# Two K tiles of a two-layer decode kernel come by strided transfers of 64 to 8 rows

## The chip, the cores and the metric

The kernel runs on one core of a Trainium2 chip. The time is that of the device, in microseconds (us), from one launch. The core has five engines with instruction queues of their own: TensorE (PE), VectorE (DVE), ScalarE (ACT), GpSimd (POOL) and SyncE (SP), and 16 DMA engines that carry transfers between the chip's memory and the core's SBUF of 128 partitions. In this kernel SP issues every transfer.

## What is computed

Two layers with the same weights are run for one new token in each of B = 2 sequences. A layer is a cached attention and then an MLP mixer:

```python
x = x + _A_ref(_layernorm(x), K, V, wq, wo)
x = x + _B_ref(_layernorm(x), w1, w2, w3, w4)

def _A_ref(x, k_cache, v_cache, wq, wo):          # D = 576, H = 32, Dh = 128, Sk = 16384
    q = (x @ wq).reshape(B, 1, H, Dh).transpose(0, 2, 1, 3)
    scores = einsum("bhqd,bhkd->bhqk", q, k_cache) * Dh ** -0.5
    o = einsum("bhqk,bhkd->bhqd", softmax(scores), v_cache)
    return o.transpose(0, 2, 1, 3).reshape(B, 1, H * Dh) @ wo
```

The mixer `_B_ref` is a layer norm, a D x D product and gelu, a shift along a sequence of length one, a second D x D product, and then a layer norm, D x 4608, gelu and 4608 x D. All data are bfloat16. The K and V caches are the bulk: for each of the 64 pairs of sequence and head there is a K and a V of 16384 x 128 values, 4 MB each, and both layers read the same caches.

## The kernel before

**Tiles.** One pair (b, h) is a unit u = 0..63. Its K is one tile, its V another. A tile of 4 MB is laid on the 128 partitions as `(p j) d -> p (j d)`: partition p gets rows 128p to 128p + 127 of the cache, which is one run of 32 KB in memory and 32 KB in SBUF. SBUF holds six such tiles (`NSLOT`, `TILE`) in the tensor `mem`. Some tiles at the ends of a layer are cut along the columns into pieces, and a few tiles of layer 0 stay in SBUF for layer 1 (`CARRY`).

**Transfers.** `plan_all` (L499) makes one list, in the order in which the transfers will be issued: wq and w2, the tiles of layer 0 in the order K0, K1, V0, K2, V1, ... (`tile_order`, L569), the weights wo, w3, w4, wq, the tiles of layer 1, and the last weights with w1. `plan_tile` (L426) and `plan_piece` (L435) put a tile on this list with its slot, its semaphore and a list of (destination, source) pairs; one pair is one transfer:

```python
        sem = f"tile{base // self.TILE}" if n == self.NB else f"piece{base // self.TILE}_{a}_{n}"
        self.store.plan((t, u, a, n), sem, base + 256 * a, 256 * n,
                        [(lambda m: m, src[:, a * 128:(a + n) * 128])])
```

`Store.pump` (L286) takes the list's head whenever its place in SBUF is free. It issues in order and never passes a transfer whose place is still in use. `Graph.dma` (L88) makes of each pair one `dma_start` on SP, all pairs of one tile on the same semaphore (L101); a reader waits for the sum, 16 for each transfer. So SP's queue is: wait until PE has read the tile that was in the slot before, issue, go on to the next tile.

**Compute.** For each unit, in turn: K arrives; PE transposes 64 of its 128 columns of blocks in chunks of eight (L1241), ACT copies them out of PSUM (L1253), PE multiplies by q (L1267); DVE does the other 64 blocks by a multiplication and a sum (L1287, L1291). DVE and POOL find the maximum, ACT takes the exponential (L1319, L1322), and PE multiplies by V one unit later (L1361). PE, ACT and DVE run most of this in loops of three units; SP's and POOL's queues are written out. POOL relays the landing of a tile to PE and DVE (L202). Between the layers the weights come in small pieces through two slots, each waiting for PE to have used the one before.

Of the kernel before, what the change touches and what calls it, by code (L numbers as in the profile page):

```python
# [328 lines left out]
class KB:  # L329
# [11 lines left out]
    PARKED = 5  # L341
    GONE = 72
    RAW = 2
    TURNS = {("w3", 0): 1, ("w3", 1): 1, ("w3", 2): 1, ("w4", 1): 1, ("w4", 3): 1, ("w4", 6): 1, ("w4", 8): 1,
             ("wq", 0): 1, ("wq", 1): 1, ("wq", 2): 1}

# [25 lines left out]
    def _alloc(self):  # L372
# [44 lines left out]
        self.quad = misc[:, 20:24]  # L417
        self.raw = misc[:, 24:24 + self.RAW * (1 + 3 * B) // 2].bitcast(BF16).rearrange("p (k c) -> p k c", k=self.RAW)
        self.cor = [self.prod[:, 1280 + 2 * MT * B * i:1280 + 2 * MT * B * (i + 1)].bitcast(FP32) for i in range(2)]
# [3 lines left out]
        self.mps = ps("mps", [128, 512], FP32)  # L423


    def plan_tile(self, t, u, slot, cuts=(), skip=0):  # L426

        b, hh = u % self.B, u // self.B
        src = (self.K if t == "k" else self.V)[b, hh].rearrange("(p j) d -> p (j d)", p=128)
        cuts = [0, *cuts, self.NB]  # L430
        for a, z in zip(cuts[:-1], cuts[1:]):
            if a >= skip:
                self.plan_piece(t, u, slot * self.TILE, src, a, z - a)

    def plan_piece(self, t, u, base, src, a, n):  # L435
        sem = f"tile{base // self.TILE}" if n == self.NB else f"piece{base // self.TILE}_{a}_{n}"
        self.store.plan((t, u, a, n), sem, base + 256 * a, 256 * n,
                        [(lambda m: m, src[:, a * 128:(a + n) * 128])])

    def plan_cols(self, nm, l, w, parts):  # L440

# [57 lines left out]
    def plan_all(self):  # L499

        T, U, n = self.TILE, self.U, self.KT - 1
        row, w3r, wqr = 2 * self.D, 2 * self.F, 2 * 128 * self.H
        H, MT = self.H, self.MT
        self.parts = {}
        self.plan_cols("wq", 0, self.wq, self.whole(self.wq, [4 * T + wqr * k for k in range(self.KT)]))
        self.plan_small("w2", 0, self.w2, 4 * T + wqr * n + wqr // 2, (0, 64))

        tiles = self.tile_order(0)
        place = [i % 6 for i in range(len(tiles))]
        place[-1] = 2  # L510
        half, quarter = self.BP, self.BP // 2
        for (t, u), slot in zip(tiles, place):
            self.plan_tile(t, u, slot, (half, half + quarter) if (t, u) == ("v", U - 1) else ())
        last = {tile: slot for tile, slot in zip(tiles, place)}
        third = U - self.CARRY - 1
        assert last["k", third] == 1 and last["v", third] == 4

        self.cuts = {}
        P = 4 * row
        a, c = [4 * T + P * i for i in range(4)], [T, T + P]  # L520
        assert 256 * self.GONE == 4 * P and 256 * 8 * self.PARKED >= 2 * P and 256 * 8 * self.NKT >= P
        turn = iter([*a, c[0]] + [a[0], a[1], c[1], a[2], a[3], c[0]] * 6)
        h = MT // 2
        self.cuts["wo", 0] = [(i, i + 4, next(turn)) for i in range(0, 32, 4)]
        halves = lambda n: [(k, m, z, next(turn)) for k in range(self.KT - 1) for m, z in ((0, n), (n, 2 * n))] + \
                           [(self.KT - 1, 0, 2 * n, next(turn))]
        w3 = halves(h)
        self.groups = [(0, 4, 8, 12, 16, 18), (0, 8, 12, 16, 18)]
        g = self.groups[0]
        self.cuts["w4", 0] = [(h * i + p, h * i + q, next(turn)) for i in range(2) for p, q in zip(g[:-1], g[1:])]  # L530
        self.plan_rows("wo", 0, self.wo, self.cuts["wo", 0])
        self.plan_cols("w3", 0, self.w3, w3)
        self.plan_groups("w4", 0, self.w4, self.cuts["w4", 0])
        self.plan_cols("wq", 1, self.wq, halves(H // 2))

        b, hh = third % self.B, third // self.B
        tiles = self.tile_order(1)
        b2, h2 = tiles[0][1] % self.B, tiles[0][1] // self.B
        for i in (1, 2, 3, None, 0):
            if i is None:  # L540
                self.plan_piece(*tiles[0], T, self.K[b2, h2].rearrange("(p j) d -> p (j d)", p=128), 0, quarter)
            else:
                self.plan_piece("v", third, 4 * T, self.V[b, hh].rearrange("(p j) d -> p (j d)", p=128),
                                i * self.GONE // 4, self.GONE // 4)
        place = [(3, 4, 5, 0, 2, 1)[i % 6] for i in range(len(tiles))]
        for i, (t, u) in enumerate(tiles):
            if (t, u) != ("v", third):
                self.plan_tile(t, u, place[i], (quarter, half, half + quarter) if i == 0 else
                               (half,) if i == len(tiles) - 1 else (), 0 if i else quarter)
        self.cuts["wo", 1] = [(0, 11, 2 * T), (11, 22, 2 * T + 11 * row), (22, 32, 0)]  # L550
        at = 10 * row
        w4_at = T + 2 * w3r + w3r // 2
        self.cuts["w4", 1] = [(0, 8, w4_at)] + \
                             [(a, b, 3 * T + (a - 8) * row) for a, b in ((8, 16), (16, 26), (26, 30), (30, 34), (34, 36))]
        self.plan_rows("wo", 1, self.wo, self.cuts["wo", 1])
        self.plan_cols("w3", 1, self.w3, self.whole(self.w3, [at, at + w3r, T, T + w3r, T + 2 * w3r]))
        self.plan_groups("w4", 1, self.w4, self.cuts["w4", 1])
        w1_at = 2 * T
        for i, k in enumerate((0, 2)):
            self.store.plan(("w1", 1, i), f"w1_{i}", w1_at + k * row, 2 * row, [  # L560
                (lambda m: m.rearrange("p (k n) -> p k n", n=self.D),
                 self.w1[k * 128:(k + 2) * 128, :].rearrange("(k p) n -> p k n", p=128))])
        self.store.plan(("w1", 1, 2), "w1_2", w1_at + 4 * row, row, [(lambda m: m[self.TL:, :], self.w1[4 * 128:, :])])
# [168 lines left out]
    def unscaled(self):  # L732

        R, B = self.RAW, self.B
        hi, lo = self.raw[:, :, 1:1 + B], self.raw[:, :, 1 + B:1 + 2 * B]
# [4 lines left out]
    def cols_chunk(self, w, l, k, out, pk, n, rhs, rk, cols, first, last=False, held=False):  # L740
# [15 lines left out]
        if l == (1 if w == "wq" else 0):  # L756
            self.turn(self.TURNS.get((w, k), 0), settle=not held)

# [60 lines left out]
    def hs_projection(self):  # L819
# [16 lines left out]
        self.copy_psum(self.hs, "hs")  # L836
        B, R = self.B, self.RAW
        self.dv(lambda e: e.tensor_copy(out=self.raw[:, :, 1 + 2 * B:], in_=self.hs[:, 0:R, :]),
# [22 lines left out]
    def rows_projection(self, w, l, rhs, rk):  # L861
# [4 lines left out]
        for i, (a, b, _) in enumerate(cuts):  # L866
# [14 lines left out]
            if l == 0:  # L881
                if (w, i) == ("wo", 1):
                    self.park(self.order(0)[self.U - self.CARRY - 1], self.NKT, self.PARKED)
                self.turn(self.TURNS.get((w, i), 0))

    def z_projection(self, l):
        B, KT, MT, R = self.B, self.KT, self.MT, self.RAW
        MB, w = MT * B, 1 + 3 * B
# [568 lines left out]
```

## Time and profile before

| | |
|---|---|
| median of 3 runs | 2550.42 us (2550.4 to 2551.58) |
| profiled execution | 2549.84 us, its span 2548.1 us |
| read from memory | 1092.37 MB, 429 GB/s over the span |
| busy share of the span | PE 63%, PE weight loads 62%, DVE 74%, ACT 47%, POOL 2% |
| transfers by size | 124 K tiles and 123 V tiles of 4096 KB, 76 smaller ones |
| issue to landing, median | K tile 40.7 us, V tile 49.6 us |

The profile page is of one execution. Its second part cuts the span into 40 slices of 63.7 us, with a digit for each engine (tenths busy), the share of the 16 DMA engines and the GB/s they moved. Its fourth part follows the chain of work that ended last back from the end: a "DMA" step there is from a transfer's issue to its landing. A row with SPq is an instruction of SP's queue that issues a transfer: start, duration, line, engine, form, what goes where. In a table of windows each engine has its busy us and count, then the granted TensorE clock, the share of the DMA engines and GB/s.

### The profile page before, as it was taken

Reading aid. Unit: us, or ns where it says so; the run is one execution under the profiler, and the core shown is the slowest. Engines: PE = TensorE matmul, PEld = TensorE weight load, DVE = VectorE, ACT = ScalarE, POOL = GpSimd, SP = SyncE. Lnnn points to the kernel's source line nnn. Section 1 sums busy time; section 2 is a strip of 40 time slices with the busy share of each in tenths; the row PEclk is TensorE's granted clock in tenths of the full one; section 3 lists DMA queues with packets and bytes.
Section 4 is the critical chain, followed back from the end, with each engine's and each line's share of the span. In section 5 each row is a group of like instructions: output and inputs, shape, how many; then the busy total and the mean of one; then the engine's idle time right before and its main releaser. Section 6 shows DMA issues by size and latency. Waiting matters only on the chain.

```text
span 2548.1 us, 74893 instructions
## 1 busy us (share of the span) xinstructions
PE 1614.7 (63%) x34407; PEld 1580.7 (62%) x34407; DVE 1897.0 (74%) x2062; ACT 1204.2 (47%) x1810; POOL 53.5 (2%) x151
## 2 busy tenths in 40 slices
PE   4666666656666666666777766656665666666566
PEld 3666666656666665666667666656665665666566
DVE  5877777777777777777648877777777777777774
ACT  3544544444454444445435544444454444445442
POOL 0000000000000000000000000000000000000000
PEclk8555555555555555555656555565555555555555
DMA  9999999999999999999999999999999999999999
GB/s 410 428 433 431 432 432 431 433 431 433 430 432 432 432 432 431 433 431 432 419 411 427 432 431 432 432 432 432 432 432 432 432 432 432 432 433 431 433 431 386
DMA packets 46928, 1093.19 MB, mean 429 GB/s; under 512 B 5140, under 2 KB 6296, under 8 KB 12440
## 3 DMA queue, kind: packets, MB, share of 16 engines
q1 hardware_dynamic: 46872, 1092.40, 100.0%
q8 instruction: 41, 0.67, 0.1%
q14 instruction: 15, 0.12, 0.0%
HBM read 1092.37 MB, written 0.00 MB: 429 GB/s over the span
## 4 chain that ended last, share of the span: by engine, by line
DMA 66%; DVE 23%; PE 5%; issue 5%; SPq 1%; ACT 0%; DVEq 0%; POOLq 0%
DMA mem<-in_A_k_cache_dram 63%; DVE s_dve L1291 12%; DVE prod L1287 9%; PE tps L1241 2%; PE mps L1361 2%; DMA mem<-in_B_w_dram 1%; DMA mem<-in_A_wo_dram 1%; PE sps L1267 1%; SPq L101 1%; PE sps L1212 1%; DVE diag L1208 0%; DVE l L1339 0%; DVE q_col L1205 0%; DMA mem<-in_A_wq_dram 0%; DVE mx L1302 0%
## 5 line engine op out<-in xcount | busy, mean ns | idle before, releaser
L1253 ACT ACTIVATE kt<-tps 128x1024 bf16<-128x1024 bf16 x992 | 1002.9, 1023 | 878.0 <-PE tps L1241 859.5
L1291 DVE TENSOR_REDUCE s_dve<-prod 128x16 f32<-128x2048 bf16 x504 | 1152.1, 2286 | 17.3
L1241 PE MATMUL tps<-ident,mem 128*128 128x128 bf16 x8192 | 1000.0, 300 | 141.3 <-POOLq L202 135.2
L1287 DVE TENSOR_TENSOR prod<-mem,qb 128x2048 bf16<-128x2048 bf16 x504 | 616.8, 1224 | 525.4 <-POOLq L202 493.9
L1361 PE MATMUL mps<-p,mem 128*128 128x1 bf16 x16384 | 512.2, 166 | 549.7 <-POOLq L202 519.3
L1241 PEld LDWEIGHTS tps<-ident,mem 128*128 128x128 bf16 x8192 | 761.3, 136 | 151.1 <-POOLq L202 145.0
L1361 PEld LDWEIGHTS mps<-p,mem 128*128 128x128 bf16 x16384 | 487.5, 104 | 558.3 <-ACT p L1322 552.2
L1267 PEld LDWEIGHTS sps<-q_col,kt 128*128 128x128 bf16 x7936 | 399.5, 113 | 0.8 <-ACT kt L1253 0.4
L1267 PE MATMUL sps<-q_col,kt 128*128 128x1 bf16 x7936 | 388.1, 170 | 0.4 <-issue 0.3
L1212 PE MATMUL sps<-diag,ones_bf 128*128 128x128 bf16 x127 | 36.5, 287 | 195.4 <-DVE diag L1208 195.4
L1212 PEld LDWEIGHTS sps<-diag,ones_bf 128*128 128x128 bf16 x127 | 13.2, 104 | 205.6 <-DVE diag L1208 205.6
L1316 ACT ACTIVATE mx<-mx 128x1 f32<-128x1 f32 x128 | 26.0, 203 | 236.2 <-POOL mx L1307 236.2
L1307 POOL PARTITION_ALL_REDUCE mx<-mx x128 | 51.1, 400 | 2441.9 <-DVE mx L1305 2323.7
L1215 ACT ACTIVATE qb<-sps 128x128 bf16<-128x128 f32 x127 | 35.2, 277 | 137.3 <-PE sps L1212 137.3
L1319 ACT ACTIVATE p<-s_dve,mx 128x64 bf16<-128x64 f32 x126 | 43.8, 348 | 4.1
L1253 ACT ACTIVATE mem<-tps 128x1024 bf16<-128x1024 bf16 x32 | 32.0, 1025 | 22.0 <-PE tps L1241 19.6
L1322 ACT ACTIVATE p<-sps,mx 128x64 bf16<-128x64 f32 x128 | 37.7, 294 | 0.1
L1302 DVE TENSOR_REDUCE mx<-sps 128x1 f32<-128x64 f32 x128 | 27.6, 216 | 7.5 <-PE sps L1267 7.5
L874 PE MATMUL mps<-prod,mem 128*128 128x2 bf16 x680 | 22.1, 166 | 14.5 <-DMA mem<-in_B_w_dram 8.8
L1208 DVE TENSOR_SCALAR diag<-ident,q_f 128x128 bf16<-128x128 bf16 x127 | 31.1, 245 | 0.0
L874 PEld LDWEIGHTS mps<-prod,mem 128*128 128x128 bf16 x680 | 20.6, 105 | 16.2 <-DMA mem<-in_B_w_dram 7.5
L707 ACT ACTIVATE misc<-misc 128x2 f32<-128x2 f32 x8 | 2.4, 296 | 51.4 <-DVE misc L705 51.4
(117 smaller groups left out, 293.4 us busy)
## 6 DMA issues: line engine op xcount, KB each, us to landing
mem<-in_A_k_cache_dram SPq DMA_DIRECT2D x124, 4096.0 KB, 40.7
mem<-in_A_v_cache_dram SPq DMA_DIRECT2D x123, 4096.0 KB, 49.6
mem<-in_B_w_dram SPq DMA_DIRECT2D x21, 576.0 KB, 7.7
mem<-in_B_w_dram SPq DMA_DIRECT2D x7, 1152.0 KB, 33.9
mem<-in_A_v_cache_dram SPq DMA_DIRECT2D x3, 2048.0 KB, 40.4
mem<-in_A_wq_dram SPq DMA_DIRECT2D x10, 512.0 KB, 6.5
mem<-in_A_wo_dram SPq DMA_DIRECT2D x8, 576.0 KB, 19.3
mem<-in_A_wq_dram SPq DMA_DIRECT2D x4, 1024.0 KB, 8.0
```

The lines of the kernel that those rows point to most:

```text
L874: ins = pe.matmul(self.mps[:, t * B:(t + 1) * B], lhsT=buf[:, o:o + 128], rhs=rhs(k), start=(k == 0 and t == 0), stop=(k == last), skip_gr ...
L1212: self.pe(lambda pe: pe.matmul(qps, lhsT=self.ones_bf[:, :], rhs=self.diag[:, :], start=True, stop=True, skip_group_check=True), reads=["o ...
L1215: self.act(lambda e: e.activation(out=self.qb[i][:, :], in_=qps, func=ACT.Copy), reads=[("qps", i)], writes=[("qb", i)], sig=("qb", i))
L1241: ins = pe.transpose(self.tps[t][:, j * 128:(j + 1) * 128], buf[:, j * 128:(j + 1) * 128], self.ident[:, :])
L1253: self.act(lambda e: e.activation(out=out, in_=self.tps[t][:, :], func=ACT.Copy), reads=[("tps", t)], writes=keys, sig=("evac", c, t, k))
L1267: ins = pe.matmul(self.sps[sp][:, c * self.CH + j:c * self.CH + j + 1], lhsT=buf[:, j * 128:(j + 1) * 128], rhs=self.q_col[:, sp:sp + 1], ...
L1287: self.dv(lambda e: e.tensor_tensor(out=prod, in0=buf.rearrange("p (j d) -> p j d", d=128), in1=qbc, op=ALU.mult), reads=[("qb", r)] + key ...
L1291: self.dv(lambda e: e.tensor_reduce(out=sd[:, c0:c0 + DB], in_=prod, axis=AX.X, op=ALU.add), reads=["prod"], writes=[("s_dve", r)], sig=(" ...
L1307: self.pool(lambda e: e.partition_all_reduce(mx[3], mx[2], channels=128, reduce_op=ROP.max), reads=[("mx2", i)], writes=[("mx3", i)])
L1319: self.act(lambda e: e.activation(out=p[:, n:self.NB], in_=self.s_dve[i][:, 0:self.NB - n], func=ACT.Exp, bias=mx[4], scale=self.scale, ac ...
L1322: self.act(lambda e: e.activation(out=p[:, 0:n], in_=self.sps[i][:, 0:n], func=ACT.Exp, bias=mx[4], scale=self.scale, accum_out=self.ls[:, ...
L1361: ins = pe.matmul(self.mps[:, 448:449], lhsT=buf[:, j * 128:(j + 1) * 128], rhs=p[:, col:col + 1], start=b == 0, stop=b == self.NB - 1, sk ...
```

## The change

Two of the tiles get a number, their share: K of unit 40 in layer 0 has 2, K of unit 20 in layer 1 has 1. A tile with a share no longer comes by one transfer of its 128 rows (partitions) but by several, each of evenly spaced rows. `runs` makes the list: rows in steps of 2, 4 and 8 (64, 32 and 16 rows) as the binary digits of 8 - share say, and what is left as runs of eight rows with a step of 16.

- Share 2: 64 rows with step 2 from 0, 32 rows with step 4 from 1, and 8 rows with step 16 from 3, 7, 11 and 15. Six transfers.
- Share 1: 64 rows with step 2 from 0, 32 rows with step 4 from 1, 16 rows with step 8 from 3, and 8 rows with step 16 from 7 and 15. Five transfers.

The first one waits for the slot as before; the others follow on SP without a wait. All of them count on the slot's semaphore. Every row goes to the partition that it went to before, and nothing changes on PE, DVE, ACT and POOL. By the change's own words half of the DMA engines move ten (nine) rows of such a tile and half six (seven), instead of eight each.

```diff
+    SHARE = {(0, "k", 40): 2, (1, "k", 20): 1}
...
-    def plan_tile(self, t, u, slot, cuts=(), skip=0):
+    def plan_tile(self, l, t, u, slot, cuts=(), skip=0):
...
             if a >= skip:
-                self.plan_piece(t, u, slot * self.TILE, src, a, z - a)
+                self.plan_piece(t, u, slot * self.TILE, src, a, z - a, self.SHARE.get((l, t, u), 0))
 
-    def plan_piece(self, t, u, base, src, a, n):
+    @staticmethod
+    def runs(share):
+
+        out, free = [], list(range(16))
+        if not share:
+            return [slice(0, 128)]
+        for n, step in ((4, 2), (2, 4), (1, 8)):
+            if (8 - share) & n:
+                at = free[0]
+                out.append(slice(at, 128, step))
+                free = [r for r in free if (r - at) % step]
+        return out + [slice(r, 128, 16) for r in free]
+
+    def plan_piece(self, t, u, base, src, a, n, share=0):
         sem = f"tile{base // self.TILE}" if n == self.NB else f"piece{base // self.TILE}_{a}_{n}"
         self.store.plan((t, u, a, n), sem, base + 256 * a, 256 * n,
-                        [(lambda m: m, src[:, a * 128:(a + n) * 128])])
+                        [(lambda m, r=r: m[r, :], src[r, a * 128:(a + n) * 128]) for r in self.runs(share)])
...
-            self.plan_tile(t, u, slot, (half, half + quarter) if (t, u) == ("v", U - 1) else ())
+            self.plan_tile(0, t, u, slot, (half, half + quarter) if (t, u) == ("v", U - 1) else ())
...
-                self.plan_tile(t, u, place[i], (quarter, half, half + quarter) if i == 0 else
+                self.plan_tile(1, t, u, place[i], (quarter, half, half + quarter) if i == 0 else
```

## The prediction

> **What bounds the kernel now.** I read the page from its head down, then one stretch of the steady part, then the two places where the transfers are not steady (the change from layer 0 to layer 1, and the end). The page first: the busy lines, the two DMA lines of the slices, the packets, the queue, the chain.
>
> ```profile
> span 2548.1 us, 74893 instructions
> PE 1614.7 (63%) x34407; PEld 1580.7 (62%) x34407; DVE 1897.0 (74%) x2062; ACT 1204.2 (47%) x1810; POOL 53.5 (2%) x151
> ...
> DMA  9999999999999999999999999999999999999999
> GB/s 410 428 433 431 432 432 431 433 431 433 430 432 432 432 432 431 433 431 432 419 411 427 432 431 432 432 432 432 432 432 432 432 432 432 432 433 431 433 431 386
> DMA packets 46928, 1093.19 MB, mean 429 GB/s; under 512 B 5140, under 2 KB 6296, under 8 KB 12440
> ...
> q1 hardware_dynamic: 46872, 1092.40, 100.0%
> ...
> DMA 66%; DVE 23%; PE 5%; issue 5%; SPq 1%; ACT 0%; DVEq 0%; POOLq 0%
> ```
>
> The reader is to see that no compute engine passes 74%, while the 16 transfer engines are at 9 in every slice and move 431 to 433 GB/s in nearly all of them. The kernel is bound by its 1092 MB of reads; 66% of the chain is transfers. Next the queue that issues them, in the steady part, and what it waits for.
>
> ```profile
> 503.18 0.33 SPq L101 DMA_DIRECT2D mem<-in_A_k_cache_dram  x1
> 504.04 0.33 SPq L101 DMA_DIRECT2D mem<-in_A_v_cache_dram  x1
> 522.62 0.33 SPq L101 DMA_DIRECT2D mem<-in_A_k_cache_dram  x1
> ...
> SPq L101 <- PE sps L1267: 2142.2, 124, 18.6
> ...
> mem<-in_A_k_cache_dram SPq DMA_DIRECT2D x124, 4096.0 KB, 40.7
> mem<-in_A_v_cache_dram SPq DMA_DIRECT2D x123, 4096.0 KB, 49.6
> ```
>
> One K and one V tile, 8 MB, go out every 522.62 - 503.18 = 19.44 us, and SP spends 2142 us waiting for a slot that PE has read. A K tile lands 40.7 us after its issue, which is two steps of 19.44: the 40.7 is queueing, so the engines always have about four tiles before them. A tile has 128 rows, eight for each of 16 engines; two tiles are 16 rows of an engine, so **one 32 KB row costs its engine 19.44 / 16 = 1.215 us**. This is the unit of all that follows. As the engines never stand still, time that one of them loses is not made up later, and the last of the 16 sets when a tile has landed.
>
> **The change part by part.** *What it moves.* Two of 247 whole tiles no longer come by one transfer of 128 rows but by six (64, 32 and four of 8 rows) and by five (64, 32, 16 and two of 8). The bytes stay. Two transfers of the kernel have two rows (the input x and the output); the other 321 of the 323 issues in the page's last part have 64 or 128. The 5140 packets under 512 B fit 321 x 16 + 2 x 2: each engine that takes part writes one small packet at its end, and a transfer of two rows uses two engines. So one of eight rows uses eight. With the same eight each time, these move 4 + 2 + 4 = 10 rows of the first tile and 4 + 2 + 1 + 2 = 9 of the second, the other eight 6 and 7.
>
> *Issues.* Nine more on SP, at 0.33 us each: five behind the first K tile's, 1.7 us, and four behind the second's, 1.3 us. The V tile is queued behind them on SP and goes that much later; nothing waits on SP for them, as only the first part waits for the slot. Cost nothing: the cover is the queue of 40.7 us and the 2142 us that SP idles. Without the cover it would be 3.0 us. The 96 more small packets, three to nine for an engine, I cost at nothing too; they are within the 1.215 us, where each tile's eight rows have one already.
>
> *The rows, if every engine runs alone.* The heavy half ends its tile 2 x 1.215 = 2.43 us later in layer 0 and 1.215 us later in layer 1, the light half as much earlier. Both halves go straight on, so the offset stays. If the last engine before is in the heavy half, the tile lands 2.43 us later and so does all behind it: +3.65 us in sum. If the last ones are all in the light half there is a gain. What balance can give at all is bounded by the places where engines idle:
>
> ```profile
> core 0: us, PE busy (x) PEld busy (x) DVE busy (x) ACT busy (x) POOL busy (x), PEclk, DMA share, GB/s
> 500.00:600.00 100.00, 63.22 (x1327) 62.10 (x1328) 75.02 (x78) 47.20 (x72) 1.80 (x5) 0.57 1.00 431
> 1231.00:1340.00 109.00, 78.66 (x1932) 74.43 (x1930) 51.83 (x126) 45.11 (x68) 5.62 (x5) 0.56 1.01 411
> ```
>
> ```profile
> core 0 of [0], span 2548.1 us
> DMA  7999999999989899978676556555731000000000
> GB/s 324 443 387 443 387 464 422 436 401 437 383 352 398 348 415 383 376 281 338 271 285 257 218 211 229 190 186 194 244 123 56 32 7 0 0 0 0 7 0 0
> ```
>
> The second fence is the last 13.1 us (2535.0 to 2548.1), in slices of 0.33 us. From the 11th slice on the rate falls below 432, and by the 33rd it is gone: engines finish one after the other. The shortfall summed is 2.8 us, so perfect balance at the end gains at most that. Between the layers 411 instead of 431 GB/s over 109 us is 5.1 us; part of it is small packets and waits for buffers that balance does not touch. So the floor is 7.9 us below, and that needs everything.
>
> *The rows, if two engines get in each other's way.* In a whole tile an engine's rows go always to the same partitions; in rows 2 to 16 apart they needn't. No row of this trace shows a large transfer of this shape. The nearest row is the whole tile's 1.215 us, the lower end. The upper end is two engines that take turns at one place, 2.43 us a row. With all rows at the upper end the heavy half needs 10 x 2.43 instead of 8 x 1.215, +14.6 us, and 9 x 2.43, +12.1 us: +26.7 us. I take half of the rows as doubled: engines are out of step, as the ragged end shows, so pairs will partly miss each other, and neither end is nearer. That is 10 x 1.215 + 5 x 1.215 - 9.72 = **+8.5 us** for the first tile and 9 x 1.215 + 4.5 x 1.215 - 9.72 = **+6.7 us** for the second. I keep the ends 0 and +26.7.
>
> The Trainium skill, page "SBUF — State Buffer", section "Door 1: The DMA port swizzle", says that transfers reach SBUF by 16 ports, each belonging to eight partitions that are not neighbours, and that the number of ports reached sets the rate: by its table 64 neighbouring partitions load hardly faster than 32. By that rule an 8-row transfer with a step of 16 reaches only four ports, two rows on each, and its eight engines go at half rate, an estimate that is this part's upper end for those rows; no run here shows it. With only these rows doubled (four and two of the heavy half) the sum by that rule would be 2549.84 + 3.65 + 6 x 1.215 = 2560.8 us. [...]
>
> *Who waits.* The K tile that lands late holds DVE and PE for its lateness, and behind them the release of a slot and SP's next issue. DVE works 75.02 of 100 us, so it makes up 25% of 19.44 = 4.9 us in each step, and 8.5 us are gone within two; the queue of 40.7 us covers SP's lateness meanwhile. The engines' own lost time is not covered: they are at 1.00.
>
> *The sum.* 2549.84 (the profiled execution: span 2548.1 and 1.7 around it; the median of the runs is 0.58 higher) + 8.5 + 6.7 + 0 for issues = **2565.0 us**.
>
> **The rivals.** *Engines run alone (33 in 100).* Then only the offsets count: 2549.84 - 1.2 to + 3.65, that is 2548.6 to 2553.5, within 0.2% (5.1 us, about what a measurement of this kernel can tell from no change). For it: every row of a whole tile costs the same 1.215 us all through the steady part, so the engines do not disturb each other there. Against it: there each has its own partitions, and this is just what is given up. It decides if the strided rows still cost 1.215 us.
>
> *Balance wins (5 in 100).* The ragged end means that some engines are ahead. If the eight that get more are just those, and the strided rows cost nothing more, the end gives back up to 2.8 us and the change of layers some of its 5.1 us: 2550 - 2.8 - 3 = 2544. It needs more than 5.1 of the 7.9 us, thus nearly a perfect fit at both places, with shifts of 2.43 and 1.215 us. Speaking for it: the end falls in two stages, first to 5 or 6 tenths and then to nothing, which looks like two groups. Against it: the offset of layer 0 is 4.86 us between the halves, more than the whole tail can use.
>
> *The V tile behind is late (2 in 100).* If the queue were shallower than it looks, the 1.7 and 1.3 us of issues would show as idle engines: 2552.9. The 40.7 us speak against it.
>
> **How the numbers follow.** Crowded rows have 60 in 100. Within them the cost runs from 5.1 us to 26.7 us, so their own range is 2555 to 2576.5, with 2565.0 in the middle. Engines alone have 33, the late V tile 2, both within 0.2%; balance 5. Faster by over 0.2%: 0.05. Within: 0.33 + 0.02 = 0.35. Slower by over 0.2%: 0.60. The range must reach the second case: 2549.0 leaves out the balance case and a few in 100 of the engines alone; 2576.5, the full doubling, leaves out another few, for the case that three engines meet at one place.
>
> **What would show it.** Packets under 512 B 5140 + 6 x 16 = 5236 if the 8-row transfers use eight engines each. In the issue table 122 whole K tiles, two parts of 2048 KB and six of 256 KB. The step of the first split tile lands about 8.5 us late by the crowded case (the chain's DMA piece 49 instead of 40.7 us), 2.4 at most by the engines alone. DMA share stays 1.00 while the GB/s of the slice of 63.7 us that has the tile falls by 8.5 / 63.7 = 13%, if all engines lose as much, and less if the light half doesn't; by the engines alone it stays at 431 to 433. The change of layers should hide little of it: the stretch from 1231 to 1340 moves as a whole. The prediction is wrong if that slice keeps 432 GB/s, if the tail's raggedness and not the tile sets the time, or if the layers' change, where buffers and not engines set the pace, takes the first 8.5 us in.

## The result and the profile after

The changed kernel takes 2567.2 us (median of 6 runs, 2565.52 to 2569.09) against 2550.32 us before: ratio 1.0067, interval 1.0055 to 1.0079, so 16.9 us slower. 2565.0 was predicted. The profiled execution after, the fastest of the six, has a span of 2563.8 us, 15.7 more than before. The page after, the same lines as before:

```profile
span 2563.8 us, 74902 instructions
...
DMA  9999999999999999999999999999999999999999
GB/s 409 431 431 432 431 431 432 431 432 430 433 432 385 432 431 431 433 431 433 405 411 428 430 432 433 432 390 431 432 432 433 430 433 431 433 433 430 433 431 381
DMA packets 47024, 1093.19 MB, mean 426 GB/s; under 512 B 5236, under 2 KB 6392, under 8 KB 12536
```

The reader is to see two new dips, 385 and 390 GB/s, in the two slices of 64.1 us that hold the split tiles, while the DMA engines stay at 9 tenths: they are busy, but they move less. The packets under 512 B are 5236, as foretold for transfers of eight rows that use eight engines.

Next the stretch around each split tile. First two windows of the kernel before, at the places of the two tiles.

```profile
780.00:860.00 80.00, 51.53 (x1064) 50.63 (x1063) 61.51 (x63) 39.46 (x59) 1.42 (x4) 0.56 1.00 432
1680.00:1760.00 80.00, 49.26 (x1046) 48.40 (x1047) 61.51 (x62) 38.20 (x61) 1.61 (x5) 0.59 1.00 432
```

Then the kernel after: SP's queue, four windows (the two tiles, the heart of the first, the change of layers), the step of the chain that ends with the first tile's landing, and the transfers that SP issued between 787 and 808 us, with their median from issue to landing.

```profile
755.68 3.68 SPq L101 DMA_DIRECT2D mem<-in_A_k_cache_dram  x6
759.40 0.44 SPq L101 DMA_DIRECT2D mem<-in_A_v_cache_dram  x1
775.14 0.34 SPq L101 DMA_DIRECT2D mem<-in_A_k_cache_dram  x1
...
780.00:860.00 80.00, 43.34 (x910) 42.53 (x907) 55.99 (x57) 34.26 (x53) 1.42 (x4) 0.56 1.00 395
787.00:808.00 21.00, 8.07 (x194) 7.91 (x192) 6.29 (x6) 3.51 (x5) 0.00 (x0) 0.50 1.01 290
1700.00:1780.00 80.00, 45.55 (x947) 44.73 (x945) 58.16 (x58) 35.48 (x54) 1.40 (x4) 0.56 1.00 400
1241.00:1350.00 109.00, 78.71 (x1972) 74.20 (x1970) 51.58 (x125) 44.67 (x68) 5.62 (x5) 0.57 0.99 403
...
758.79 47.88 DMA mem<-in_A_k_cache_dram
...
mem<-in_A_k_cache_dram SPq DMA_DIRECT2D x1, 4096.0 KB, 50.7
mem<-in_A_v_cache_dram SPq DMA_DIRECT2D x1, 4096.0 KB, 59.6
```

In the 21 us in which most of the first tile comes the engines are at 1.01 and move 290 GB/s. This gives a measure that all the experiments below use: **the mean loss of an engine at a tile is the shortfall against 432 GB/s, over the window.** Both windows of the kernel before have 432 GB/s. Here the loss is (432 - 395) / 432 x 80 = 6.9 us for the first tile and (432 - 400) / 432 x 80 = 5.9 us for the second. The last engine loses more than the mean: tiles issued behind the split one land 50.7 and 59.6 us after their issue, not 40.7 and 49.6, 10.0 us late. The chain's transfer step ends at 758.79 + 47.88 = 806.7 us: this is the split tile, 51.0 us after its first issue.

The trace also has the time of each row, which is a packet of 32 KB. Of the 1054 rows that start between 780 and 860 us before, none takes over 1.57 us, and the median is 1.216 us. After, 88 of 963 take over 1.8 us, and the median of these is 2.46 us, twice as long. Only 32 rows of the first tile come by transfers of eight, so most of the slow rows are others. The V tile behind shows whose they are, by the times at which its semaphore counts up, once for each of the 16 engines: before from 803.1 to 806.3 us; after, eight engines from 807.2 to 810.5 and eight from 813.1 to 816.1, in the mean 4.3 and 9.3 us late. By the shares alone one half would be 2.4 us early and the other 2.4 us late. So **both halves lost about 6.8 us to slow rows**, and not the half with the more rows alone.

### The profile page after: what moved, and what is told of

It is laid out like the page before. It is cut to its first block, busy times and chain, and to the rows that moved or that the text cites. A ratio compares the mean times of both kernels' runs of the same rounds, so it can differ in the third digit from the quotient of the medians.

```text
span 2563.8 us, 74902 instructions
## 1 busy us (share of the span) xinstructions
PE 1614.6 (63%) x34407; PEld 1580.7 (62%) x34407; DVE 1897.2 (74%) x2062; ACT 1204.8 (47%) x1810; POOL 53.5 (2%) x151
## 2 busy tenths in 40 slices
DMA packets 47024, 1093.19 MB, mean 426 GB/s; under 512 B 5236, under 2 KB 6392, under 8 KB 12536
## 4 chain that ended last, share of the span: by engine, by line
DMA 66%; DVE 22%; PE 5%; issue 5%; SPq 1%; another core or an unknown queue 0%; ACT 0%; DVEq 0%; POOLq 0%; POOL 0%
DMA mem<-in_A_k_cache_dram 63%; DVE s_dve L1305 12%; DVE prod L1301 8%; PE tps L1255 2%; PE mps L1375 2%; DMA mem<-in_B_w_dram 1%; DMA mem<-in_A_wo_dram 1%; SPq L101 1%; PE sps L1281 1%; PE sps L1226 1%; DVE diag L1222 0%; DVE l L1353 0%; DVE q_col L1219 0%; DVE mx L1316 0%
## 5 line engine op out<-in xcount | busy, mean ns | idle before, releaser
L888 PE MATMUL mps<-prod,mem 128*128 128x2 bf16 x680 | 22.2, 166 | 12.8 <-DMA mem<-in_B_w_dram 7.8
L1314 DVE TENSOR_REDUCE mx<-s_dve 128x1 f32<-128x64 f32 x126 | 26.3, 209 | 0.0
## 6 DMA issues: line engine op xcount, KB each, us to landing
mem<-in_A_v_cache_dram SPq DMA_DIRECT2D x123, 4096.0 KB, 49.6
mem<-in_A_k_cache_dram SPq DMA_DIRECT2D x122, 4096.0 KB, 40.7
```

Source lines behind the costliest of these rows:

```text
L888: ins = pe.matmul(self.mps[:, t * B:(t + 1) * B], lhsT=buf[:, o:o + 128], rhs=rhs(k), start=(k == 0 and t == 0), stop=(k == last), skip_gr ...
```

## Experiments

All of them change only how the two tiles are cut: K of unit 40 in layer 0 (the first) and K of unit 20 in layer 1 (the second). `rows(n, step)` stands for a whole tile in transfers of n rows that lie step apart. The kernel before of the same chip had medians of 2550.18 us (for the first seven kernels) and 2550.47 us (for the last three), with single times from 2549.48 to 2550.88. Kernels without an interval here were timed once. In the diffs `...` stands for lines left out.

**One tile at a time.**

```diff
-    SHARE = {(0, "k", 40): 2, (1, "k", 20): 1}
+    SHARE = {(0, "k", 40): 2}          # and, in the other run, {(1, "k", 20): 1}
```

> Only layer 0's tile with share 2. If the two tiles' costs simply add, and the change of layers hides little, this is 9 to 10 us over the kernel before (the last engine's loss at the tile) and the other one 8. If the change of layers takes in the offset between the halves, it is nearer to the engines' mean loss in the stretch, (432 - 290) / 432 x 21 = 6.9 us.

> Only layer 1's tile with share 1. Nothing behind it but the end of the kernel can take in an offset: 8 us over the kernel before if the last engine is in the heavy half, (432 - 286) / 432 x 18 = 6.1 us if the offset evens out the end. With the run that has only layer 0's tile the sum should be the change's 16.9 us.

Measured: 2559.09 us with the first alone (ratio 1.0037, interval 1.0024 to 1.005), +8.9 us; 2557.48 us with the second alone (1.0029, 1.0018 to 1.0041), +7.3 us. The sum is 16.2 where the change has 16.9. So the costs add. The first lies between the mean loss of 6.9 us and the last engine's 10.0: the change of layers hides about 1 us of it.

**Is it the number of transfers?**

```diff
+    SHARE = {(0, "k", 40): 6, (1, "k", 20): 1}
...
+        cuts = [0, 64, 96, 104, 112, 120, 128][:share] + [128]
+        return [(slice(0, 128), slice(128 * a, 128 * z), src) for a, z in zip(cuts[:-1], cuts[1:])]
```

> Layer 0's tile by six transfers, as in the change, but each of all 128 rows and of a part of the columns (rows of 16, 8 and four times 2 KB); layer 1's tile whole, by one. If it is the number of transfers or the five issues more on SP that cost, this loses as much as the change's first tile: its stretch at about 290 GB/s for 21 us. If it is the rows' places, nothing: 432 GB/s and the time of the kernel before, within 1 us for the smaller packets.

Measured: 2550.13 us, and the first tile's window:

```profile
780.00:860.00 80.00, 50.79 (x1070) 49.90 (x1068) 61.16 (x62) 39.15 (x59) 1.42 (x4) 0.57 1.01 430
```

0.4 us lost, none in the time. Six transfers and five more issues are free, so the cost is in the rows' places.

**Is it the uneven share, or any strided transfer?**

```diff
+    SHARE = {(0, "k", 40): (64, 2), (1, "k", 20): (64, 1)}
...
+        return [(r, c, src[r, :]) for r, c in rows(*share)]
```

> Both tiles come evenly, eight rows for each engine, by two transfers of 64 rows: layer 0's with rows 0, 2, 4, ... and 1, 3, 5, ..., layer 1's with rows 0 to 63 and 64 to 127. A row of a whole tile costs its engine 1.215 us. If only the uneven share costs (10 rows against 6), both tiles cost nothing: 432 GB/s in both stretches, the time of the kernel before. If rows crowd at their destination, the layer 0 tile costs between 0 and 8 x 1.215 = 9.7 us, as the engines are out of step, and the layer 1 tile 9.7 us, together 10 to 19 us over the kernel before. If the distance of the rows in the source costs, the layer 0 tile loses time and the layer 1 tile, whose rows lie together, nothing. By the Trainium skill, page "SBUF — State Buffer", section "Door 1: The DMA port swizzle", 64 neighbouring partitions reach 8 of 16 ports; by that rule the layer 1 tile goes at half the rate throughout, an estimate.

Measured: 2563.99 us, and the two tiles differ as much as can be:

```profile
780.00:860.00 80.00, 51.27 (x1065) 50.38 (x1063) 61.51 (x63) 39.42 (x59) 1.42 (x4) 0.56 1.00 431
1680.00:1760.00 80.00, 40.84 (x870) 40.21 (x871) 51.60 (x51) 30.87 (x49) 1.27 (x4) 0.54 1.00 355
```

Every second row: 0.2 us lost, nothing. 64 neighbouring rows: (432 - 355) / 432 x 80 = 14.3 us lost, though the share is even (5172 packets under 512 B, 32 more than before, fit 16 engines for every one of the four transfers). So "strided" is not what costs, and an even share does not protect. No row of the first window is slow; in the second 183 rows take over 1.8 us, more than the tile's 128, so rows of the tiles beside it are slowed as well. The page "SBUF — State Buffer" of the Trainium skill, section "Door 1: The DMA port swizzle", has half the rate for 64 neighbours; that would be 9.7 us, an estimate, and the measured loss is half as much again.

**Source or destination?** In the first run the first tile's rows are neighbours in the cache and go to partitions two apart; the second tile comes whole, to all 128 partitions, but from rows 16 apart in the cache. In the second run transfers of eight rows go to partitions 16 apart from neighbouring rows (first tile), and to partitions 4 apart from rows 16 apart (second tile). Where source and destination differ, the tile holds other keys than its unit asks for; the work is the same.

```diff
+    SHARE = {(0, "k", 40): "near", (1, "k", 20): "far"}
...
+        if share == "near":             # first tile
+            return [(slice(h, 128, 2), slice(None), src[64 * h:64 * h + 64, :]) for h in range(2)]
+        far = self.K[0, 0:16].rearrange("h (p j) d -> (h p) (j d)", p=128)
+        return [(slice(0, 128), slice(None), far[0:2048:16, :])]
```

> The source and the destination taken apart. Layer 0's tile: two transfers of 64 rows, in SBUF on every second partition, in the cache 64 neighbouring rows each. Layer 1's tile: one transfer of 128 rows to all partitions, as before, but read from rows 16 apart (512 KB), thus from other units. Both tiles have other keys than the reference asks for, so the result differs; the work on all engines is the same. If the destination costs, the first tile costs what the same tile costs with both sides strided (layer 0 of the run with halves), and the second nothing: 432 GB/s and 9.7 us. If the source's distance costs, it is the other way: 432 GB/s at the first, and up to 9.7 us lost at the second, as a row would take 2.43 instead of 1.215 us.

```diff
+    SHARE = {(0, "k", 40): "to", (1, "k", 20): "of"}
...
+        near = [src[8 * i:8 * i + 8, :] for i in range(16)]
+        far = [src[i:128:16, :] for i in range(16)]
+        to, of = ((8, 16), near) if share == "to" else ((8, 4), far)
+        return [(r, c, s) for (r, c), s in zip(rows(*to), of)]
```

> Source and destination taken apart for the transfers of eight rows, 16 for each tile. Layer 0's tile: to partitions 16 apart, from eight neighbouring rows. Layer 1's tile: to partitions 4 apart, from rows 16 apart. Both tiles hold other keys than the reference asks for; the work is the same. With both sides alike, 16 apart lost 31.4 us for each engine in the mean and 4 apart (432 - 366) / 432 x 80 = 12.2. If the destination sets it: about 31 in layer 0 and 12 in layer 1. If the source sets it: about 12 in layer 0, or less, and 31 in layer 1. If both sides take part, both lie between.

Measured: the first run 2549.69 us, 431 and 432 GB/s in the tiles' windows: nothing lost.

```profile
780.00:860.00 80.00, 51.32 (x1065) 50.43 (x1063) 61.50 (x63) 39.51 (x59) 1.42 (x4) 0.56 1.00 431
1680.00:1760.00 80.00, 49.16 (x1046) 48.30 (x1047) 61.50 (x62) 38.12 (x61) 1.60 (x5) 0.56 1.00 432
```

Since 64 rows two apart cost nothing anyway, its first tile decides nothing; its second shows that 128 rows 512 KB apart are read at full rate. The page "DMA: Bandwidth & Descriptors" of the Trainium skill, section "Latency and other measured facts", has 207 GB/s at this distance beside 214 as full, for copies of 16 KiB rows between tensors in HBM; 432 GB/s here agrees that it costs little. The second run, 2617.66 us, decides. Its windows:

```profile
780.00:860.00 80.00, 18.24 (x397) 17.96 (x395) 26.75 (x28) 15.53 (x25) 0.70 (x2) 0.52 1.00 234
1720.00:1840.00 120.00, 62.95 (x1313) 61.84 (x1312) 75.87 (x77) 47.53 (x71) 1.75 (x5) 0.54 1.00 386
```

To partitions 16 apart, from neighbouring rows: 36.7 us lost. To partitions 4 apart, from rows 16 apart: 12.8 us. With both sides alike (next) it was 31.4 and 12.2. For transfers of eight rows the loss follows the destination.

**The price of each form.**

```diff
+    SHARE = {(0, "k", 40): (16, 8), (1, "k", 20): (16, 1)}      # and {(0, "k", 40): (8, 4), (1, "k", 20): (8, 16)}
```

> Both tiles evenly by eight transfers of 16 rows, one row for each engine at a time: layer 0's 8 apart, layer 1's neighbours. If the destination costs by groups of partitions, neighbours are worse: with four engines at one place a row takes 4 x 1.215 = 4.86 us, eight rows 38.9 us instead of 9.7, so 29 us lost by each engine; 8 apart two engines meet, up to 9.7 us lost, less what they miss each other by. If the source's distance costs, the neighbours cost nothing and the rows 8 apart (256 KB) lose time. If it is the number of transfers (eight each) both cost the same. By the Trainium skill, page "SBUF — State Buffer", section "Door 1: The DMA port swizzle", 16 neighbouring partitions reach four ports and 16 that lie 8 apart eight; these two figures are behind the four and the two engines at one place.

> Both tiles by 16 transfers of eight rows: layer 0's 4 apart, layer 1's 16 apart. First: packets under 512 B. If a transfer of eight rows uses eight engines, each tile adds 16 x 8 - 16 = 112, and the page has 5140 + 224 = 5364. If they are the same eight each time, these move 16 rows a tile and the others none: at 1.215 us a row 19.4 us, so at least 9.7 us lost by them for each tile and as much gained by the others, and the last lands 9.7 us late. If the destination costs by groups, the rows 16 apart take twice as long where those 4 apart do not: 38.9 against 19.4 us for the eight engines, thus 29 against 9.7 us late. If the source's distance costs (512 KB against 128 KB) the order is the same, so this run does not tell these two apart; it tells the number of engines and the size for the transfers of eight rows, of which the change has six.

Measured: 2584.02 and 2617.51 us. The windows of both tiles, first of the run with 16 rows, then of the one with eight:

```profile
780.00:860.00 80.00, 39.40 (x827) 38.75 (x825) 51.76 (x55) 32.34 (x51) 1.42 (x4) 0.59 1.01 359
1700.00:1800.00 100.00, 50.61 (x1061) 49.72 (x1058) 61.94 (x64) 38.49 (x59) 1.41 (x4) 0.55 1.01 353
```

```profile
780.00:860.00 80.00, 37.04 (x772) 36.37 (x771) 44.27 (x46) 27.88 (x43) 1.07 (x3) 0.54 1.00 366
1720.00:1840.00 120.00, 46.81 (x1001) 46.09 (x1002) 55.50 (x56) 34.57 (x54) 1.40 (x4) 0.55 1.00 319
```

16 rows 8 apart lost 13.5 us (9.7 at most was expected), 16 neighbours 18.3 (29 expected): the neighbours are worse, as by the destination, but by far less than four engines in turn at one place would make them. In the second run eight rows 4 apart lost 12.2 us in the mean, 16 apart 31.4. Its packets under 512 B are 5364, as expected. And the eight engines are the same each time: the V tile behind its first split tile ends on eight engines from 793.5 to 799.1 us, on the other eight from 825.0 to 828.2. It shows at the end too, in the last two slices:

```profile
GB/s 409 430 432 432 432 431 432 431 432 431 433 431 353 432 431 431 432 432 431 354 415 428 432 430 431 433 251 400 432 431 432 432 432 432 430 432 432 432 423 302
```

423 and 302 at the end, where the kernel before has 431 and 386, as engines that are ahead have finished. In layer 0 the same stands at the change of layers (354 in the 20th slice, 419 before).

One thing more lies in the first tile of this run. Its 16 transfers have one form, eight rows 4 apart; the first eight go to partitions 0 to 63, the others to 64 to 127. The same window in two parts:

```profile
783.00:792.00 9.00, 3.98 (x96) 3.92 (x96) 8.86 (x10) 3.56 (x8) 0.35 (x1) 0.66 1.01 433
795.00:812.00 17.00, 0.50 (x19) 0.41 (x16) 0.00 (x0) 0.52 (x1) 0.00 (x0) 0.50 0.99 204
```

No row that starts in the first part, when the lower partitions are written, takes over 1.23 us. Every row that starts in the second, when the upper ones are written, takes 2.46 to 2.57 us, also those of the other eight engines, which are already at the tiles behind. The second tile of the run before, in the same order of partitions but from other rows, has the same two parts: 430 GB/s from 1743 to 1752 us, 209 from 1755 to 1773. So the form of a transfer does not set the price by itself; it depends on the partitions.

**The forms of the change without eights.**

```diff
+    SHARE = {(0, "k", 40): 4, (1, "k", 20): 1}
...
+        if share == 4:
+            return [(r, c, src[r, :]) for r, c in rows(32, 4)]
+        return [(r, slice(None), src[r, :]) for r in (slice(0, 128, 2), slice(1, 128, 4), slice(3, 128, 8), slice(7, 128, 8))]
```

> The forms of the change without its transfers of eight rows, all even. Layer 0's tile: four transfers of 32 rows, 4 apart. Layer 1's tile: 64 rows 2 apart, 32 rows 4 apart, and two times 16 rows 8 apart. So far 64 rows 2 apart lost nothing, eight transfers of 16 rows 8 apart (432 - 359) / 432 x 80 = 13.5 us for each engine in the mean, 1.7 each, and 16 of eight rows 16 apart (432 - 319) / 432 x 120 = 31.4 us, 2.0 each. If each form has its price and 32 rows have none, the first tile loses 0 and the second 2 x 1.7 = 3.4 us. Then the change's first tile is 4 x 2.0 = 8 (6.9 measured) and its second 1.7 + 2 x 2.0 = 5.7 (5.9 measured). If 32 rows 4 apart also cost, the first tile shows it: more than 2 us.

Measured: 2556.59 us. The windows:

```profile
780.00:860.00 80.00, 51.19 (x1064) 50.30 (x1062) 61.52 (x62) 39.38 (x59) 1.42 (x4) 0.56 1.00 431
1680.00:1760.00 80.00, 48.70 (x1028) 47.88 (x1028) 55.99 (x54) 35.83 (x55) 1.27 (x4) 0.55 1.00 401
```

Four transfers of 32 rows 4 apart: 0.2 us, nothing. Two of 16 rows 8 apart: 5.7 us, where 3.4 were expected from the price of eight of them. The price of a form is not a constant: 2.9 us each here, 1.7 there. But the split is clear: 64 rows and 32 rows of these spacings are free, and rows are slow only while the change's transfers of 16 and eight rows are under way.

**Another spacing.** Same shares, same number of transfers, the eights 4 apart.

```diff
+        first = [slice(0, 128, 2), slice(1, 128, 4)]
+        last = [slice(r, min(128, r + 32), 4) for r in (3, 35, 67, 99)]
+        if share == 1:
+            last = [slice(3, 67, 4), *last[2:]]
+        return [(r, slice(None), src[r, :]) for r in first + last]
```

> The change with the same shares and the same number of transfers, but the transfers of eight rows take rows 4 apart instead of 16: layer 0's 64 and 32 as in the change and four times eight rows 4 apart; layer 1's 64 and 32, then 16 rows 4 apart and two times eight. Sixteen transfers of eight rows 4 apart lost 12.2 us for each engine in the mean, 0.8 each. If the spacing sets the price, the first tile loses 4 x 0.8 = 3 us instead of 6.9 and the second 2 x 0.8 and a price for 16 rows 4 apart, some 2: 3.3 instead of 5.9, and the whole is 6 to 9 us over the kernel before instead of 17. If the uneven share itself has a gain under the crowding, this comes out below 6 us. If the price is one for any transfer of eight rows, it stays at 17.

Measured: 2563.07 us, ratio 1.0054 (1.0036 to 1.0072), +12.6 us: between the 6 to 9 us of the one theory and the 17 of the other. The windows:

```profile
780.00:860.00 80.00, 44.89 (x986) 44.07 (x985) 56.66 (x59) 35.06 (x55) 1.42 (x4) 0.59 1.00 411
1690.00:1770.00 80.00, 47.22 (x990) 46.30 (x988) 54.91 (x53) 36.28 (x51) 1.05 (x3) 0.56 1.01 404
```

The first tile loses 3.9 us in the mean instead of 6.9; the second 5.2 instead of 5.9. In the first tile only two of the four transfers of eight go to partitions 64 to 127, and the slow rows begin at about 793 us, when the first two are through. The time grows by more than these 9.1 us: the half that is ahead then waits at the change of layers and at the end. Of the two uneven cuts tried, neither costs nothing, and neither gains.

The tiles cut in one form, side by side (mean loss of an engine for a tile that takes 9.7 us when whole):

| cut | loss, us |
|---|---|
| 128 rows, six parts by columns | 0.4 |
| 2 x 64 rows, 2 apart | 0.2 |
| 4 x 32 rows, 4 apart | 0.2 |
| 8 x 16 rows, 8 apart | 13.5 |
| 2 x 64 neighbouring rows | 14.3 |
| 8 x 16 neighbouring rows | 18.3 |
| 16 x 8 rows, 4 apart | 12.2 |
| 16 x 8 rows, 16 apart | 31.4 |

## Why the prediction was right, and where it was not

- **The bound and the unit** held. Nearly all slices of whole tiles have 430 to 434 GB/s in every kernel, and time that the engines lose at one tile is in the end in the kernel's time. The mean losses of 6.9 and 5.9 us, 2.0 us more of idle engines at the change of layers (403 GB/s where 411 were, over 109 us) and 1.0 us at the end (366 where 375 were, over 48 us) make 15.8 us; the span grew by 15.7.
- **Issues**: put at nothing, though at 0.33 us each. Six took 3.68 us (0.61 each), and the V tile went out 3.7 us after the first. It cost nothing: the run by columns has the same six and no loss. The rival of the late V tile falls.
- **Engines run alone** falls: 88 rows around the first tile took over 1.8 us, not 1.215. **Balance wins** falls: at both tiles engines lost time on average, where balance would only have shifted it, and both single tiles are slower. The end was not mended: the last slice has 381 GB/s, where 386 were.
- **Crowded rows** is what happened, and the sum was near: +8.5 and +6.7 foretold, +8.9 and +7.3 measured for the tiles alone. The upper price, 2.43 us for a row, was right too: the slow rows' median is 2.46. The step that failed inside it is "half of the rows as doubled". The number is near: the first tile's heavy half was to lose five rows' worth, 6.1 us, and lost 6.8. But it is not a random half, and engines out of step are not the reason. 64 and 32 rows cost nothing, so six rows of each heavy engine run at full rate, or nearly; the rows by eights are the ones that go at half rate, and with them the rows that the other half moves at the same time. That the sum fits is thus in part luck.
- **The light half**: for engines that run alone it was to be "as much earlier"; for crowded rows the prediction left open whether it loses, and the sum took only the heavy half. It was 4.3 us late: having two rows fewer saved it 2.4 us, and slow rows cost it 6.8. The smaller sum of 2560.8 us, in which only the heavy half's rows by eights are doubled, leaves this out too.
- **Destination, not source**: the prediction put the cost at the partitions. That is shown by the run that takes the two apart, for transfers of eight rows; the distance in memory costs nothing at 512 KB.
- **The change of layers** "moves as a whole": nearly. It takes about 1 us out of the first tile's 10.0, and its own stretch loses the 2.0 us above: the lighter half waits there for the heavier one. Ahead of it the halves still end a tile apart, eight engines from 1205.5 to 1208.8 us and eight from 1211.4 to 1214.4; behind it all 16 end one from 1365.4 to 1368.4.
- **The slices** were foretold at -13% if all engines lose, and are at -11% (385) and -10% (390); the landing at 49 us, and it was 51.0 from the tile's first issue.

Shown is that rows take twice as long in both halves of the engines, that this depends on the partitions written, and, for transfers of eight rows, that it does not depend on the source. That two engines meet at one place is inferred, from the doubled time. Open: which partitions an engine writes in each form, and why two transfers of 16 rows 8 apart cost 2.9 us each and eight of them 1.7. For 16 and for 64 neighbouring rows source and destination were not taken apart.

## What to carry to other kernels

When the transfer engines are busy all the time, look at GB/s beside their share: a share of 1.00 with fewer GB/s means that the same engines move less, here because of where their rows went. Cutting a tile by columns, or in strides that spread 32 or 64 rows over all partitions, cost nothing here; a tile of 9.7 us cut into transfers of 16 or eight rows, or of 64 neighbouring rows, lost 12 to 37 us. Moving rows from one engine to another did not balance the load: the engines that got fewer rows were late as well, by 4.3 us at the first tile.

## What was not expected of the hardware

- Eight rows 4 apart go at 1.22 us a row to partitions 0 to 63, and at 2.5 us to 64 to 127; there they slow the other eight engines' rows just as much.
- An even cut into 64 neighbouring rows costs 14.3 us, more than a full doubling of the tile's 9.7 us, while 64 rows two apart and 32 rows four apart cost 0.2 us.
- 16 neighbouring rows cost 18.3 us, not much more than 16 rows 8 apart (13.5 us).
- A whole tile read from rows 512 KB apart comes at 432 GB/s, like one from neighbouring rows.
- An issue takes 0.33 us alone and 0.61 us in a row of six.
